# A gated block with sliding-window attention on one core: maxima and denominators go from SBUF to SBUF, and transfers that follow other engines are issued later

## The chip, the cores and the metric

The kernel runs on one core of a Trainium2 chip. The core has TensorE (matmuls, in the profile PE, its weight loads PEld), VectorE (DVE), ScalarE (ACT), GpSimd (POOL) and SyncE (SP), which issues nearly all transfers. [...] The metric is the device time of one execution in microseconds, the median of several runs.

## The reference

`x` is 2048 x 512. It is normalised by rows, and the result feeds two branches: causal attention over a window of 256 positions with 32 heads of 16, and a feed-forward network with a silu gate of width 1792. The output is the input plus attention times silu of the network's output.

```python
xn = _layernorm(x, axis=-1)
# s = _A_ref(xn, A_wqkv, A_wo)
scores = jnp.einsum("bhqd,bhkd->bhqk", q, k) * (Dh ** -0.5)
mask = (idx[:, None] - idx[None, :] >= 0) & (idx[:, None] - idx[None, :] < W)
scores = jnp.where(mask[None, None], scores, -1e9)
p = _softmax(scores, axis=-1)
o = jnp.einsum("bhqk,bhkd->bhqd", p, v)
return (lambda x, *d: x.transpose(*d))(o, 0, 2, 1, 3).reshape(B, S, D) @ wo
# g = _silu(_B_ref(xn, B_w1, B_w3, B_w2))
h = _silu(gate) * up
out = jnp.einsum("bsf,fd->bsd", h, w2)
# the output
return x + s * g
```

## The kernel before

**Tiles and units.** The 2048 positions are four blocks `t` of 512, the 32 heads four groups `g` of eight. A pair (t, g) is a *tile*; each tile has two *units* p of four heads, so there are 32 units, some 22 us each from the third on. Float32 accuracy is kept by splitting operands into two half-precision parts, hi and lo, and taking three products.

**Two passes a unit.** Pass 1 (L643) computes scores with queries on the partitions, adds the mask and takes the row maximum on VectorE (L675) into `M`. `negate` (L684) writes the negated maxima as two half-precision terms into `nm`. `finish` (L690) turns them on TensorE, VectorE copies them to `mt` (L700), and they become two more rows of the query tile `qa`, rows 64r+48 and 64r+49, so that the second score product subtracts the maximum by itself. `mt` is [32, 128], its rows in the order (term b, row half r, piece i). Pass 2 (L720) makes the scores again with the keys on the partitions (L741), masks them (L748), takes exp on ScalarE (L751), and multiplies with V, to which a column of ones is joined (L769): 16 rows of values and one of denominators for each head. `os` (L784, L785) collects these from PSUM, and its rows 16, 48, 80 and 112 are the denominators.

**From `os` to the attention output.** Four transfers (L791) gather the values of a unit into `on` [128, 512], head by head; one (L792) writes the denominators to a scratch tensor `dd` in HBM. When both units of a tile are done, `normalise` (L803) reads `dd` back as `dr` [128, 32] (L807), so that the reciprocal (L812, L813) runs over 128 partitions; the result goes to HBM as `de` (L815) and comes back eight times, broadcast to 16 partitions each, as `rb` (L819). GpSimd multiplies `on` by `rb` (L820, seen under the helper's line L339) and `cut` (L822) splits the product into the two parts that the output projection `total` (L1278, L1298) reads. `on`, `rb` and `os` have one buffer each, `qa` three.

**The feed-forward network** runs between the pieces of attention: `gate_up` (L1010, L1021), its products L1040 and L1045 on VectorE, the way down `down` (L1234, L1246) in blocks 0 and 1. In blocks 2 and 3 the way down is done with seven products in place of eight (`fold_first`, `fold_second`, `fold_down_piece`, L1164), on sums that GpSimd makes (L1079, L1102 to L1104); the folded weights are computed in block 1 by `fold_weights` (L960), written to `dFold` (L997) and read back by `load_fold` (L1141). Block 0 cuts each weight matrix into its parts and stores them in HBM, the later blocks load these (L849, L895, L628).

**What sets the order.** TensorE's instructions run in the order of the program text (`ORDERED`). For the other engines and for SyncE's queue, a scheduler picks the order when the program is built, by when it reckons that each instruction is ready and by priority; each engine then works strictly in that order, and waits at an instruction whose input has not come, with the rest of its queue behind it. `urgent()` (L138) raises the priority, `tc.issue_after` places an instruction behind a named one. The program text itself is a list of pieces of about six matmuls. `step()` (L148) counts them in `now`, and `later(n, f)` (L144) places the code of `f` n steps further on. A *slot* is a buffer of 2 KB a partition out of a pool of 55: `take` (L113) gives out the slot that was returned with the earliest time stamp, and `give(..., after=n)` (L120) stamps it n steps ahead, so that slots whose last reader is late are used again later. An instruction that writes a slot still waits for its last reader to be done.

The main loop (L1602) runs one unit after the other: pass 2 of unit n, with pass 1 of unit n + 2 and pieces of projections, values, output and network spread between. After each even unit, `fetch` (L630, L637, called at L1622) loads keys and queries of the tile whose pass 1 begins one unit later.

Of the kernel before, what the change touches and what calls it, by code (L numbers as in the profile page):

```python
# [51 lines left out]
VB = 10  # L52
SLOTS = 55
ORDERED = {ENGINE.PE}
# [29 lines left out]
def tile_block(ctx: ExitStack, tc: tile.TileContext, x, wqkv, wo, w1, w3, w2, out):  # L84
# [558 lines left out]
    def pass1(t, g, p):  # L643
# [40 lines left out]
        def negate():  # L684
            Mf = M.rearrange("p r a i -> p (r a i)")
            with tc.issue_after(lasts["emptied"].ins):
                nc.vector.tensor_scalar(nm[:, 0, :], Mf, -1.0 / ONE, None, op0=ALU.mult)
                nc.vector.scalar_tensor_tensor(nm[:, 1, :], Mf, -1.0 / ONE, nm[:, 0, :], op0=ALU.mult, op1=ALU.subtract)

        def finish(s):  # L690

            for h in range(2):
                rows = slice(64 * h, 64 * h + 64)
                nc.tensor.matmul(s[0:64, h, 448:512], whole[rows, 0:64], identh[rows, rows], start=True, stop=True)

            def rest():
                qa = QA[t, g]
                mt = small.tile([32, P], F16, name="mt")
                with urgent():
                    nc.vector.tensor_copy(mt.rearrange("p (h q) -> p h q", h=2), s[0:32, :, 448:512])  # L700
                dm = dpool.tile([32, P], F16, name="dm")
                nc.sync.dma_start(dm, mt)
                for r in range(2):
                    nc.sync.dma_start(qa[64 * r + KR:64 * r + KR + 2, 2 * p:2 * p + 2, :].rearrange("p a q -> p (a q)"),
                                      dm.rearrange("(b r i) q -> r b (i q)", b=2, r=2)[r])
            return rest
# [13 lines left out]
    def pass2(t, g, p):  # L720
# [54 lines left out]
        def finish():  # L775
# [3 lines left out]
            def rest():  # L779
# [6 lines left out]
                if p == 0:  # L786
                    ON[t, g] = (opool.tile([P, TW], F32, name="on", bufs=1), dpool.tile([8, TW], F32, name="dd"))
                on, dd = ON[t, g]
                for i in range(4):
                    h = (i // 2) * 4 + 2 * p + i % 2  # L790
                    nc.sync.dma_start(on[16 * h:16 * h + 16, :], os[32 * i:32 * i + 16, :])  # L791
                nc.sync.dma_start(dd[4 * p:4 * p + 4, :], os[DH::32, :])  # L792
                if p == 1:
# [9 lines left out]
    def normalise(t, g):  # L803
        on, dd = ON.pop((t, g))
        last = (t, g) == tiles[-1]
        dr = small.tile([P, 32], F32, name="dr")
        nc.sync.dma_start(dr, dd.rearrange("h (b c) -> (h b) c", c=32))  # L807
        rb = opool.tile([P, TW], F32, name="rb", bufs=1)

        def invert():  # L810
# [4 lines left out]
            nc.sync.dma_start(de.rearrange("h (b c) -> (h b) c", c=32), dr)  # L815
            for i in range(8):
                p, r, a = i // 4, i // 2 % 2, i % 2
                h = r * 4 + 2 * p + a
                nc.sync.dma_start(rb[16 * h:16 * h + 16, :], de[i:i + 1, :].to_broadcast([16, TW]))  # L819
            halves(nc.gpsimd.tensor_mul, on, on, rb)  # L820

# [138 lines left out]
    def fold_weights(j):  # L960
# [22 lines left out]
        def cut(raw, n, kind):  # L983
# [11 lines left out]
            def store():  # L995
                with behind_load():
                    nc.sync.dma_start(dFold[kind, :, j, 0:2 * n], a[:, 0:2 * n])  # L997
                give(a, after=30)
            later(8, store)

# [9 lines left out]
    def gate_up(t, f):  # L1010
        cell = {}

        def part(k, half):
# [28 lines left out]
            else:  # L1042
# [10 lines left out]
                def rest():  # L1053
                    nc.scalar.copy(hh[:, 0:TW], sg)  # L1054
                    halves(nc.gpsimd.tensor_sub, hh[:, TW:], sg, hh[:, 0:TW])
                    give(sg, after=8)
                later(1, rest)
# [220 lines left out]
    def total(t, b):  # L1278
# [4 lines left out]
        def part(half):  # L1283
# [16 lines left out]
            if half:  # L1300
# [4 lines left out]
                else:  # L1305
                    halves(nc.gpsimd.tensor_add, y, y, XR[t, b])
                nc.sync.dma_start(out[r, :], y)
                give(y, XR[t, b], after=6)
                if b == 3:
# [292 lines left out]
    for n, u in enumerate(units):  # L1602
# [18 lines left out]
        if n % 2 == 0 and k < len(tiles):  # L1621
            later(1, lambda k=k: fetch(*tiles[k]))  # L1622
    for b in (1, 3):
# [32 lines left out]
```

## Time and profile before

| | |
|---|---|
| Median of 3 runs | 815.16 us (814.53 to 816.15) |
| The profiled execution | 816.52 us, of which the span from first to last instruction is 814.7 us |
| Granted TensorE clock, mean | 0.999 |
| Moved by DMA | 134.71 MB, 165 GB/s over the span; the main queue took 55.6% of the 16 engines |
| Transfers issued by SyncE for maxima | 32 `dm<-mt` of 8 KB, 64 `qa<-dm` of 4 KB |
| for denominators | 32 `dd<-os` of 8 KB, 16 `dr<-dd` of 16 KB, 16 `de<-dr` of 16 KB |
| for values and factors | 128 `on<-os` and 128 `rb<-de`, 32 KB each |

How the rows of the profile are read: an engine's row names the line, what is written and read (`out<-in`), shapes and counts; "idle before" is the time in which that engine stood still ahead of the instruction, and the name behind the arrow is what ended it. SyncE computes nothing, so its rows are the issuing of transfers, and its waits are those of the whole queue. A matmul's busy time includes the part in which the next one already streams, so TensorE is marked busy a little longer than it is. Lines inside a helper stand for all its callers: L339 is every half-tile operation on GpSimd, and the tile names tell which.

### The profile page before, as it was taken

To read this page: it belongs to the slowest core of one execution; us is meant where nothing else is said; L and a number is where in the kernel's file an instruction comes from. 1 tells how busy PE (TensorE), PEld (TensorE's weight loads), DVE (VectorE), ACT (ScalarE), POOL (GpSimd) and SP (SyncE) were. 2 spreads that over 40 slices of the span, in tenths; PEclk is the share of its full clock that TensorE was granted. 3 is DMA by queue.
4 is the path that set the end of the run, shared out by engine and by line. 5 is a ranking of instruction groups with operands and counts; after the bars stand their busy time and mean duration, and the time that the engine had idled before them with its cause. 6 is when DMAs were issued, how large, how long until landed. Compare 5 with 4: busy or idle time off the path is not lost.

```text
span 814.7 us, 23924 instructions
## 1 busy us (share of the span) xinstructions
PE 794.2 (97%) x9176; PEld 404.0 (50%) x9176; DVE 636.6 (78%) x2037; ACT 392.5 (48%) x591; POOL 366.6 (45%) x648
## 2 busy tenths in 40 slices
PE   8999989999999999999999999999999999999997
PEld 4444444444444444444445444456544654466465
DVE  8788888888888768887988888586777887875537
ACT  6879596653546544345443443344344234344411
POOL 2234265333339447155253454530246276550671
PEclk9999999999999999999999999999999999999999
DMA  9979764666652576747556453755653653226511
GB/s 283 254 244 301 246 206 137 229 186 177 189 146 82 157 241 196 214 128 216 164 145 170 124 147 79 190 159 160 171 151 85 159 167 112 87 67 181 163 38 64
DMA packets 109923, 134.71 MB, mean 165 GB/s; under 512 B 18736, under 2 KB 64752, under 8 KB 109808
## 3 DMA queue, kind: packets, MB, share of 16 engines
q1 hardware_dynamic: 109520, 132.66, 55.6%
q8 instruction: 72, 1.18, 0.6%
q10 hardware_dynamic: 288, 0.52, 0.2%
q14 instruction: 43, 0.35, 0.1%
HBM read 91.75 MB, written 37.09 MB: 158 GB/s over the span
## 4 chain that ended last, share of the span: by engine, by line
PE 67%; DVE 12%; DMA 7%; ACT 6%; issue 3%; POOL 3%; SPq 1%; DVEq 0%; POOLq 0%; ACTq 0%
PE m L1021 25%; PE m L1164 8%; PE po L769 8%; PE m L1246 6%; PE m L593 6%; PE s L741 4%; DVE junk L675 3%; PE m L563 3%; PE m L1298 3%; PE s L661 2%; DVE s L748 2%; DMA slot<-dW 1%; PE po L661 1%; ACT pt L751 1%; DMA dm<-mt 1%
## 5 line engine op out<-in xcount | busy, mean ns | idle before, releaser
L1021 PE MATMUL m<-XH,slot 128*128 128x512 f16 x896 | 267.3, 380 | 1.9 <-DVE slot L614 1.2
L751 ACT ACTIVATE pt<-s,es 128x1024 f32<-128x1024 f32 x152 | 167.7, 1113 | 194.1 <-DVE s L748 182.6
L339 POOL TENSOR_TENSOR slot<-slot,slot 128x256 f16<-128x256 f32 (+1 forms) x170 | 113.3, 695 | 203.8 <-ACT slot L1054 75.6
L1021 PEld LDWEIGHTS <-slot 128*128 128x128 f16 x1344 | 124.9, 98 | 156.2 <-issue 12.6
L1021 PE MATMUL m<-XL,slot 128*128 128x512 f16 x448 | 169.8, 379 | 0.0
L748 DVE TENSOR_TENSOR s<-s,MK 128x256 f32<-128x256 f32 (+2 forms) x280 | 118.7, 434 | 50.9 <-PE s L741 45.7
L675 DVE CUSTOM_DVE_ANT_0 junk<-s,MW 128x320 bf16<-128x320 f32 x276 | 133.8, 485 | 17.6 <-PE s L661 10.2
L675 DVE CUSTOM_DVE_ANT_0 junk<-po,MW 128x320 bf16<-128x320 f32 x172 | 83.4, 485 | 4.2
L1246 PE MATMUL m<-slot,slot 128*128 128x512 f16 x336 | 78.7, 380 | 1.3 <-DVE slot L1040 0.9
L769 PE MATMUL po<-pt,V 64*32 64x320 f32 (+4 forms) x2880 | 77.2, 342 | 0.8 <-DVE pp L304 0.8
L593 PE MATMUL m<-XH,slot 128*128 128x512 f16 x240 | 70.9, 380 | 1.2 <-DVE slot L614 0.6
L1164 PE MATMUL m<-slot,slot 128*128 128x256 f16 x588 | 68.4, 273 | 0.0
L1079 POOL TENSOR_TENSOR slot<-slot,slot 128x256 f16<-128x256 f32 x98 | 64.7, 673 | 1.2
L1036 ACT ACTIVATE slot<-m,sgs 128x512 f32<-128x512 f32 x56 | 38.2, 683 | 54.8 <-PE m L1021 49.8
L1164 PEld LDWEIGHTS <-slot 128*128 128x128 f16 x588 | 56.2, 98 | 11.4 <-issue 2.8
L769 PEld LDWEIGHTS po<-pt,V 64*32 64x32 f32 x2880 | 50.4, 106 | 23.0 <-PE s L513 0.9
L1040 DVE SCALAR_TENSOR_TENSOR slot<-slot,m 128x512 f32<-128x512 f32 x56 | 38.3, 684 | 29.0 <-ACT slot L1036 28.9
L741 PE MATMUL s<-qa,KA 50*64 50x320 f16 (+3 forms) x1472 | 58.7, 259 | 1.8 <-DMA qa<-dm 1.7
L593 PEld LDWEIGHTS <-slot 128*128 128x128 f16 x384 | 35.7, 98 | 44.5 <-issue 3.2
L741 PEld LDWEIGHTS <-KA 50*64 50x64 f16 x1472 | 30.4, 105 | 53.8 <-issue 30.7
L339 POOL TENSOR_TENSOR on<-on,rb 128x256 f32<-128x256 f32 x32 | 24.4, 786 | 66.1 <-DMA rb<-de 58.1
L1246 PEld LDWEIGHTS <-slot 128*128 128x128 f16 x336 | 30.7, 98 | 39.7 <-issue 5.6
(188 smaller groups left out, 1121.9 us busy)
## 6 DMA issues: line engine op xcount, KB each, us to landing
slot<-dW SPq DMA_DIRECT2D x98, 256.0 KB
slot<-in_B_w_dram SPq DMA_DIRECT2D x56, 256.0 KB
slot<-dFold SPq DMA_DIRECT2D x48, 256.0 KB
dW<-slot SPq DMA_DIRECT2D x42, 256.0 KB
slot<-in_A_x_dram SPq DMA_DIRECT2D x30, 256.0 KB
KA<-dK SPq DMA_DIRECT2D x24, 288.0 KB
qa<-dQ SPq DMA_DIRECT2D x32, 192.0 KB
slot<-dWQ SPq DMA_DIRECT2D x24, 256.0 KB
```

Of the source, the lines that this page charges most:

```text
L339: op(out[:, c], a[:, c], b[:, c])
L593: nc.tensor.matmul(cell["pp"], w[:, (a * NC + c) * P:(a * NC + c + 1) * P], b[:, c, :], start=(c, i) == parts[0][0], stop=(c, i) == parts[ ...
L675: lasts["maximum"] = nc.vector.tensor_tensor_reduce(out=junk[:, :n], in0=s[:, r, :n], in1=mask, scale=1.0, scalar=NEG, op0=ALU.add, op1=AL ...
L741: nc.tensor.matmul(s[64 * h:64 * h + 64, r, o:o + 64 * n], ka[rows, 2 * p + a, 64 * (m + 4):64 * (m + 5)], qa[rows, 2 * p + a, 64 * (m + k ...
L748: nc.vector.tensor_add(v, v, MK[:, kind, of:of + n, :].unsqueeze(1).to_broadcast([P, 2 * len(which), n, 64]))
L751: lasts["exp"] = nc.scalar.activation(pt, s, AF.Exp, scale=es)
L769: nc.tensor.matmul(cell["po"][32 * i:32 * i + 32, h, 64 * (m + k):64 * (m + k + n)], V[64 * h:64 * h + 64, (4 * t + m // 2) % VB, hd * VW: ...
L1021: nc.tensor.matmul(cell[k], w[:, (a * NC + c) * P:(a * NC + c + 1) * P], b[:, c, :], start=c == 0 and i == 0, stop=c == NC - 1 and i == 2)
L1040: lasts["emptied"] = nc.vector.scalar_tensor_tensor(sg, sg, 1.0, cell[0], op0=ALU.add, op1=ALU.mult)
L1079: nc.gpsimd.tensor_sub(lo, view, hi)
L1164: nc.tensor.matmul(cell["ps"][:, c], made[:, f:f + P], wj[:, g:g + 256], start=j == j0 and c == 0 and n == 0, stop=j == j1 - 1 and n == 2, ...
L1246: nc.tensor.matmul(ps, hh[:, a * TW + b * P:a * TW + (b + 1) * P], w[:, c * D:(c + 1) * D], start=f == f0 and i == 0, stop=f == f1 - 1 and ...
```

## The change

Nothing is computed in another way; transfers and their places in the text change.

- *Maxima*: the scratch `dm` goes. Four transfers a unit, marked urgent, take eight rows of `mt` each and write one row of `qa`.
- *Denominators*: the scratch `dd` goes. `gather` copies the four rows of `os` straight into half of `dr` (64 partitions of 32 numbers) and then the values into `on`, two steps later than before except in the last tile.
- *Buffers*: `on` takes the pool's two buffers in place of one; the slots go from 55 to 54, which is as much memory.
- *Factors*: the loads of `rb` and the product come three steps after the reciprocal, except in the last tile.
- *Negations* are marked urgent.
- *Later*: stores of folded weights after 14 steps (8 before), output stores after four (at once before, and still so in the last block), `fetch` after three (one before). The gate's product gives its slot back 20 steps ahead in block 1 (8 before), output and residual 30 ahead (6 before).

```diff
-SLOTS = 55
+SLOTS = 54
...
         def negate():
             Mf = M.rearrange("p r a i -> p (r a i)")
-            with tc.issue_after(lasts["emptied"].ins):
+            with urgent(), tc.issue_after(lasts["emptied"].ins):
...
-                dm = dpool.tile([32, P], F16, name="dm")
-                nc.sync.dma_start(dm, mt)
-                for r in range(2):
-                    nc.sync.dma_start(qa[64 * r + KR:64 * r + KR + 2, 2 * p:2 * p + 2, :].rearrange("p a q -> p (a q)"),
-                                      dm.rearrange("(b r i) q -> r b (i q)", b=2, r=2)[r])
+                for b in range(2):
+                    for r in range(2):
+                        row = 64 * r + KR + b
+                        with urgent():
+                            nc.sync.dma_start(qa[row:row + 1, 2 * p:2 * p + 2, :].rearrange("p a q -> p (a q)"),
+                                              mt[16 * b + 8 * r:16 * b + 8 * r + 8, :])
...
                 if p == 0:
-                    ON[t, g] = (opool.tile([P, TW], F32, name="on", bufs=1), dpool.tile([8, TW], F32, name="dd"))
-                on, dd = ON[t, g]
-                for i in range(4):
-                    h = (i // 2) * 4 + 2 * p + i % 2
-                    nc.sync.dma_start(on[16 * h:16 * h + 16, :], os[32 * i:32 * i + 16, :])
-                nc.sync.dma_start(dd[4 * p:4 * p + 4, :], os[DH::32, :])
+                    ON[t, g] = opool.tile([P, TW], F32, name="on"), small.tile([P, 32], F32, name="dr")
+                on, dr = ON[t, g]
+
+                def gather():
+                    nc.sync.dma_start(dr[64 * p:64 * p + 64, :], os[DH::32, :])
+                    for i in range(4):
+                        h = (i // 2) * 4 + 2 * p + i % 2
+                        nc.sync.dma_start(on[16 * h:16 * h + 16, :], os[32 * i:32 * i + 16, :])
+                if (t, g) == tiles[-1]:
+                    gather()
+                else:
+                    later(2, gather)
...
     def normalise(t, g):
-        on, dd = ON.pop((t, g))
+        on, dr = ON.pop((t, g))
         last = (t, g) == tiles[-1]
-        dr = small.tile([P, 32], F32, name="dr")
-        nc.sync.dma_start(dr, dd.rearrange("h (b c) -> (h b) c", c=32))
...
-            for i in range(8):
-                p, r, a = i // 4, i // 2 % 2, i % 2
-                h = r * 4 + 2 * p + a
-                nc.sync.dma_start(rb[16 * h:16 * h + 16, :], de[i:i + 1, :].to_broadcast([16, TW]))
-            halves(nc.gpsimd.tensor_mul, on, on, rb)
+
+            def multiply():
+                for i in range(8):
+                    p, r, a = i // 4, i // 2 % 2, i % 2
+                    h = r * 4 + 2 * p + a
+                    nc.sync.dma_start(rb[16 * h:16 * h + 16, :], de[i:i + 1, :].to_broadcast([16, TW]))
+                halves(nc.gpsimd.tensor_mul, on, on, rb)
+            if last:
+                multiply()
+            else:
+                later(3, multiply)
...
-            later(8, store)
+            later(14, store)
...
-                    give(sg, after=8)
+                    give(sg, after=8 if t == 0 else 20)
...
-                nc.sync.dma_start(out[r, :], y)
-                give(y, XR[t, b], after=6)
+
+                def store():
+                    nc.sync.dma_start(out[r, :], y)
+                    give(y, XR[t, b], after=30)
+                if t == NT - 1:
+                    store()
+                else:
+                    later(4, store)
...
         if n % 2 == 0 and k < len(tiles):
-            later(1, lambda k=k: fetch(*tiles[k]))
+            later(3, lambda k=k: fetch(*tiles[k]))
```

## The prediction

> **What bounds the kernel now.** I read the engine totals first, then the same in stretches of 20 us, then the list of what TensorE waited for, then SyncE's queue and the chain of waits around the one place where a transfer holds TensorE.
>
> ```profile
> PE 794.2 (97%) x9176; PEld 404.0 (50%) x9176; DVE 636.6 (78%) x2037; ACT 392.5 (48%) x591; POOL 366.6 (45%) x648
> 100.00:120.00 20.00, 17.22 (x220) 8.50 (x219) 17.65 (x69) 17.13 (x33) 12.74 (x26) 1.00 0.65 204
> 500.00:520.00 20.00, 18.23 (x229) 8.50 (x228) 15.13 (x46) 7.87 (x10) 13.71 (x23) 1.00 0.46 123
> 520.00:540.00 20.00, 19.41 (x248) 9.85 (x246) 12.96 (x40) 7.81 (x11) 9.71 (x17) 1.00 0.64 179
> 800.00:815.00 15.00, 10.37 (x59) 5.32 (x57) 11.32 (x22) 2.73 (x5) 0.88 (x1) 0.94 0.20 72
> ```
>
> The stretches give span, then TensorE, its weight loads, VectorE, ScalarE and GpSimd, then clock, DMA share and GB/s. TensorE is busy for 794.2 of 814.7 us, its clock is full, and the number and order of its matmuls do not change here. So the change can win at most part of the 20.5 us in which TensorE is idle, and of these only what a transfer or a late VectorE step causes: some 2.8 us in 100 to 120, 1.8 in 500 to 520, 0.6 in 520 to 540, and the end.
>
> ```profile
> PE s L661 <- ACT pt L751: 2.1, 3, 1.0
> PE s L741 <- DMA qa<-dm: 1.7, 2, 1.5
> PE s L694 <- DVE NM L688: 1.2, 2, 1.1
> PE m L1298 <- DVE slot L827: 0.8, 1, 0.8
> PE s L661 <- DMA qa<-dQ: 0.4, 1, 0.4
> ```
>
> This view of waits (total us, times, longest) is the list of candidates. No weight load stands in it: TensorE never waits for a weight from HBM. The 1.7 us for the maxima is the one steady-state wait on a transfer, and it falls at 516 us:
>
> ```profile
> 499.82 0.27 DVE L700 CAST mt<-s 32x128 f16<-32x128 f32 x1
> 503.83 2.45 SPq L791 DMA_DIRECT2D on<-os  x4
> 509.19 0.36 SPq L1276 DMA_DIRECT2D slot<-in_A_x_dram  x1
> 510.70 0.38 SPq L702 DMA_DIRECT2D dm<-mt  x1
> ```
>
> The maxima are in SBUF at 500.1, and SyncE sends them at 510.7 only: its queue is in order, and `on<-os` ahead of them waits until 503.8 for GpSimd to be done with the one `on` buffer. The chain of waits carries on from there (start, us, what):
>
> ```profile
> 498.61 1.77 DMA rb<-de
> 510.70 2.97 DMA dm<-mt
> 513.99 2.85 DMA qa<-dm
> 523.88 3.14 DMA dd<-os
> 527.04 1.84 DMA dr<-dd
> ```
>
> Two hops in a row, 2.97 and 2.85, follow the late start and end at 516.84, under the scores of the next unit. The denominators then repeat it, 3.14 and 1.84. What SyncE itself waits for with its queue behind it:
>
> ```profile
> SPq L791 <- POOL slot L339: 34.1, 11, 5.4
> SPq L791 <- DVE os L785: 29.2, 6, 11.8
> SPq L704 <- DMA dm<-mt: 22.1, 16, 3.9
> SPq L819 <- DMA de<-dr: 19.9, 13, 3.8
> SPq L1141 <- POOL slot L1079: 15.1, 4, 10.8
> ```
>
> **The change part by part.** *Maxima.* The scratch `dm` goes; four transfers of one `qa` row each take the place of one write and two reads, marked urgent so that they go ahead in SyncE's order. That removes one hop (2.9 us) and the 22.1 us that SyncE spent waiting for `dm`.
>
> ```profile
> L704 SPq DMA_DIRECT2D qa<-dm x64: 228/251/336, 51.6 to 747.4; - x64
> L702 SPq DMA_DIRECT2D dm<-mt x32: 318/378/577, 49.0 to 745.2; - x32
> L791 SPq DMA_DIRECT2D on<-os x128: 507/581/1455, 86.4 to 783.9; - x128
> L792 SPq DMA_DIRECT2D dd<-os x32: 527/531/701, 89.7 to 784.5; - x32
> L819 SPq DMA_DIRECT2D rb<-de x128: 302/418/1680, 130.5 to 796.1; - x128
> ```
>
> Issuing was 32 x 0.378 + 64 x 0.251 = 28 us. A copy from 8 partitions into one row is not in the trace: between 0.251 (two rows) and 0.581 (16 rows from SBUF), so 128 of them cost 32 to 74 us. I take 0.53, the row from four partitions of SBUF, hence 68 us: 40 us more issuing against 22 us less waiting, spread over 32 units, about 0.6 us a unit on a queue that is not the bound. At 516 us it gives back the whole wait, 1.7 us: even if they were still held until 504, the rows would land at 504 + 4 x 0.53 + 3.0 = 509.1, while TensorE wants them 1.7 us before 516.84, at 515.1. Bounds: 0 (the urgent copies still stand behind another block until 510.7) to 1.7.
>
> [...] The row first: a hop here takes 1.77 to 3.14 us, whether it moves rows of 2 KB or of 128 bytes. [...]
>
> *Denominators.* `dd` goes; `dr` is filled straight from `os`, two copies a tile in place of three transfers: one issue less a tile, 16 x 0.38 = 6 us by the row of `dm<-mt`. Where a tile ends, one hop of 1.84 to 3.14 goes too, but the copies are put off by two steps (a step is some six matmuls, 6 x 0.22 = 1.3 us by the row of 25 below, so 2.6 us): even, except that SyncE no longer stands before an `os` that VectorE has not made (29.2 us above) and the reciprocal no longer stops VectorE:
>
> ```profile
> 528.90 0.35 DVE L812 RECIPROCAL dr<-dr 128x32 f32<-128x32 f32 x1 [3.33 <-DMA dr<-dd]
> ```
>
> Behind that reciprocal stand the masks, maxima and products of VectorE; TensorE pays for it near 533, in the 0.6 us of 520 to 540. I take 0.5 from 0 to 0.6.
>
> *Two `on` buffers, `rb` three steps later.* The 34.1 us of SyncE on the `on` buffer and the 19.9 us on `de` go. I cost both at nothing of their own: they are what makes the 1.7 us above safe. The eight `rb` loads and the product come some 4 us later; cover is the cut, due 14 steps (18 us) after the reciprocal, while three steps, eight issues and a landing take 3.9 + 8 x 0.42 + 1.77 = 9 us. Without cover TensorE would wait for the attention output up to the excess, at each of the three tiles that end a block.
>
> *The last tile.* Nothing is put off there, so the whole hop comes out:
>
> ```profile
> 782.07 2.42 SPq L791 DMA_DIRECT2D on<-os  x4
> 790.72 0.35 DVE L812 RECIPROCAL dr<-dr 128x32 f32<-128x32 f32 x1
> 798.00 2.88 POOL L339 TENSOR_TENSOR on<-on,rb 128x256 f32<-128x256 f32 x2 [4.80 <-DMA rb<-de]
> 799.47 2.72 PE L1298 MATMUL m<-slot,slot 128*128 128x512 f16 x11
> 802.21 0.68 DVE L827 TENSOR_TENSOR slot<-on,slot 128x512 f16<-128x512 f32 x1
> 802.95 5.57 PE L1298 MATMUL m<-slot,slot 128*128 128x512 f16 x25 [0.75 <-DVE slot L827]
> ```
>
> The denominators leave first, at 782.1, and land by 785.3 at the latest (3.14) instead of under a reciprocal at 790.7: five us earlier, or some two if VectorE takes the reciprocal later in its order. The product then starts at 793 to 796, not 798. TensorE's interval is (5.57 - 0.38)/24 = 0.216, its twelfth matmul would start at 799.47 + 11 x 0.216 = 801.85 and did at 802.95: 1.1 us, of which I take 1.0 (0 if the product stays behind GpSimd's other work).
>
> *Negations.* They are made urgent:
>
> ```profile
> 112.22 0.97 DVE L475 TENSOR_SCALAR slot<-slot,mv,rs 128x512 f32<-128x512 f32 x1
> 113.11 0.64 DVE L688 SCALAR_TENSOR_TENSOR NM<-M,NM 128x16 f16<-128x16 f32 x1
> ```
>
> The second negation stood behind a 0.97 us centring, and TensorE waited 1.1 us for it. VectorE is busy for 17.65 us of that stretch, so what it does first delays the rest, and L751 waits follow: I take 0.6 of the 1.2, from minus 0.3 to 1.2.
>
> *Stores, loads and releases later.* Output stores wait four steps, folded weights 14 instead of 8, `fetch` three instead of one, and slots rest longer, with one slot less. Cover for `fetch` is the whole unit between it and the first use (TensorE's only wait for `qa<-dQ` is 0.4 us, once); without it 2.6 us for each of 14 tiles. Slots are the risk, since loads that take a young slot wait for its last reader; I put 0.5 us on them and on the new order of VectorE, from minus 1 to plus 8 (the slot rival).
>
> **Sum**: minus 1.7, 0.5, 1.0 and 0.6, about 0.1 for smaller reciprocal stalls, plus 0.5: minus 3.4 us. The profiled execution took 816.52 with a span of 814.7 and 1.8 around it, so it would become 813.1; it stands 1.36 above the median of 815.16, which becomes 811.8.
>
> **Rivals.** *The next wait takes over.* The early stretch shows how: behind the wait for the negation stands the one for L751, 2.1 us in all. Only the end and a third of the rest would be kept: 1.0 + 0.9 - 0.5 = 1.4 less, 813.8, within what a measurement can tell from no change, which is 0.2%, 1.6 us. For it: VectorE and ScalarE are over 17 of 20 us busy at 100. Against: at 500 to 540 they are at 13 to 15 and 8.
>
> *Slots become too young (slower).* The place is the loads of folded weights before L1164:
>
> ```profile
> 717.81 0.34 SPq L1141 DMA_DIRECT2D slot<-dFold  x1
> 721.77 1.45 PE m L1164 x12
> ```
>
> SyncE stood 10.8 us before this load for a GpSimd cut (L1079); it lands at 717.81 + 2.97 = 720.8, one us before the stage it serves begins. With 54 slots and releases up to 24 steps later, such a load gets a slot whose reader ends later. If the 10.8 grows by half, TensorE loses 5.4 - 1.0 = 4.4 us; two of the four fold stages give 8.8, and 811.8 - 0.5 + 8.8 is about 820. It decides from 1 us of extra lateness, and makes the kernel slower than before when the losses pass 3.9. For it: the 15.1 us of such waits. Against: the added rests fall on slots that GpSimd reads late, and steer loads away from these.
>
> *The whole early part gains as well.* If SyncE's freedom also feeds ScalarE and VectorE in the first 200 us, half of the 2.8 us at 100 to 120 and the same again elsewhere go: 3 us more, 808.8.
>
> *The copies do not come first.* If the urgent mark does not move them, the wait at 516 stays at its lower bound: 813.5; it counts with the first rival.
>
> **How the numbers follow.** Forecast 0.51, next wait (with the last) 0.21, slots 0.18, early part 0.10. Faster than 813.5 holds in nearly all of the forecast and the early part and in a little of the second: 0.61. The same: most of the second, 0.18. Slower than 816.8: the slots and the rest, 0.21. The range takes 808.8 below and reaches above to 817.5, into the smaller half of the slot case; the forecast's own, by the bounds of its terms, is 809.5 to 814.
>
> **What would show it.** Right: no wait of TensorE on `qa` at 500 to 520, no idle VectorE before L812, no row of SyncE waiting for L339 at the gather, and the product `on<-on,rb` of the last tile before 797. Wrong: TensorE waiting for slots in L1164 or L1021, `qa<-mt` landing over 5 us after its first issue, or an idle sum in 100 to 200 that grows by what the end gives.

## The result and the profile after

The changed kernel takes 818.0 us (median of 20 runs, 816.36 to 819.84), the kernel before 814.88 us beside it (20 runs, 813.24 to 819.63): a ratio of 1.0037, interval 1.0027 to 1.0047. It is 3.1 us slower, where 3.4 us less were predicted, and outside the predicted range. The profiled execution took 817.82 us with a span of 816.0. Executions of one kernel differ here: of the twenty of the changed kernel, three with a mean clock of 1.000 took 816.36 to 816.39 us and seventeen with 0.996 or 0.998 took 817.49 to 819.84, so each ratio below is against runs of the kernel before on the same chip, whose medians go from 813.98 to 817.77.

The engine totals of the changed kernel, and the same stretches as before (span, TensorE, its weight loads, VectorE, ScalarE, GpSimd, clock, DMA share, GB/s), with 180 to 200 beside them:

```profile
PE 795.2 (97%) x9176; PEld 404.2 (50%) x9176; DVE 633.9 (78%) x2037; ACT 392.4 (48%) x591; POOL 364.0 (45%) x648
```

and the stretches:

```profile
100.00:120.00 20.00, 16.39 (x178) 7.69 (x178) 17.67 (x69) 15.72 (x30) 12.07 (x26) 1.00 0.62 198
180.00:200.00 20.00, 16.80 (x135) 7.13 (x129) 12.35 (x46) 4.51 (x5) 5.30 (x16) 0.91 0.50 151
500.00:520.00 20.00, 19.93 (x253) 9.44 (x251) 15.51 (x52) 8.43 (x12) 13.39 (x23) 1.00 0.35 105
520.00:540.00 20.00, 20.00 (x190) 9.65 (x186) 14.33 (x44) 9.44 (x13) 8.72 (x15) 1.00 0.73 202
```

500 to 540 has become as full as predicted. 100 to 120 lost another 0.8 us. The new hole is at 180 to 200, where the kernel before had TensorE busy for 19.61 us, and there the clock is no longer full. The same two places head the list of what TensorE waited for (total, times, longest):

```profile
PE m L1257 <- DVE slot L614: 3.2, 1, 3.2
PE s L661 <- ACT pt L752: 2.9, 3, 1.6
```

The first wait is a single one. GpSimd around it, in the kernel before:

```profile
183.94 0.20 POOL L466 TENSOR_TENSOR sq<-sq,u 128x4 f32<-128x4 f32 x1
184.23 0.22 POOL L467 TENSOR_SCALAR sq<-sq 128x4 f32<-128x4 f32 x1
...
185.65 0.20 POOL L472 TENSOR_TENSOR rs<-sq,r 128x4 f32<-128x4 f32 x1
185.98 1.59 POOL L339 TENSOR_TENSOR on<-on,rb 128x256 f32<-128x256 f32 x2
```

and in the changed one (timelines: start, duration, what, and in brackets the idle time before and what ended it):

```profile
185.47 0.20 POOL L466 TENSOR_TENSOR sq<-sq,u 128x4 f32<-128x4 f32 x1
185.80 1.42 POOL L339 TENSOR_TENSOR on<-on,rb 128x256 f32<-128x256 f32 x2
187.30 0.22 POOL L467 TENSOR_SCALAR sq<-sq 128x4 f32<-128x4 f32 x1
187.58 0.40 POOL L841 CAST slot<-on 128x256 f16<-128x256 f32 x1
...
189.37 0.67 POOL L339 TENSOR_TENSOR slot<-on,slot 128x256 f16<-128x256 f32 x1
190.12 0.19 POOL L471 TENSOR_SCALAR sq<-sq 128x4 f32<-128x4 f32 x1
190.40 0.20 POOL L472 TENSOR_TENSOR rs<-sq,r 128x4 f32<-128x4 f32 x1
```

VectorE there:

```profile
190.63 0.55 DVE L475 TENSOR_SCALAR slot<-slot,mv,rs 128x512 f32<-128x512 f32 x1 [3.40 <-POOL rs L472]
191.09 0.68 DVE L614 SCALAR_TENSOR_TENSOR slot<-m,slot 128x512 f16<-128x512 f32 x1
```

TensorE there:

```profile
191.83 2.72 PE L1257 MATMUL m<-slot,slot 128*128 128x512 f16 x6 [3.20 <-DVE slot L614]
```

The same matmuls in the kernel before (L1246 there):

```profile
187.64 1.46 PE L1246 MATMUL m<-slot,slot 128*128 128x512 f16 x6 [0.39 <-DVE slot L614]
```

In the changed kernel the next stretch, by engine, has a clock of 0.50 (third from the end):

```profile
191.56:194.98 3.42, 3.15 (x20) 1.13 (x23) 0.87 (x2) 0.00 (x0) 0.00 (x0) 0.50 0.66 207
```

L463 to L472 are ten small steps on 128 x 4 numbers, which refine the inverse deviations `rs` of block 2. Before, they ran in one go and the product `on<-on,rb` of a tile came behind. Now the product and the cut stand between them, and `rs` comes 4.9 us after L466 instead of 1.7. VectorE's centring (L475) waits for it 3.40 us, behind it the step (L614) that empties a bank of PSUM, the memory into which the matmuls write, and TensorE 3.20 us for the bank. Then comes a stretch of 3.42 us at half clock: six matmuls take 2.72 us, where they took 1.46 before.

The end went as predicted. GpSimd starts the last product at 795.23, not 798.00, and TensorE's wait inside L1309 (L1298 before) is 0.21 us:

```profile
795.23 1.41 POOL L339 TENSOR_TENSOR on<-on,rb 128x256 f32<-128x256 f32 x2
807.07 2.75 PE L1309 MATMUL m<-slot,slot 128*128 128x512 f16 x12 [0.21 <-DVE slot L1313]
```

### The profile page after: what moved, and what is told of

Same layout as the page of the kernel before. It is cut to its first block, busy times and chain, and to the rows that moved or that the text cites. A ratio compares the mean times of both kernels' runs of the same rounds, so it can differ in the third digit from the quotient of the medians.

```text
span 816.0 us, 23868 instructions
## 1 busy us (share of the span) xinstructions
PE 795.2 (97%) x9176; PEld 404.2 (50%) x9176; DVE 633.9 (78%) x2037; ACT 392.4 (48%) x591; POOL 364.0 (45%) x648
## 3 DMA queue, kind: packets, MB, share of 16 engines
q8 instruction: 72, 1.18, 0.6%
## 4 chain that ended last, share of the span: by engine, by line
PE 78%; DVE 10%; ACT 5%; DMA 3%; issue 3%; SPq 1%; POOL 1%; DVEq 0%; POOLq 0%; ACTq 0%
PE m L1032 29%; PE po L770 8%; PE m L1257 8%; PE m L1175 8%; PE m L593 7%; PE s L742 5%; PE m L1309 4%; PE m L563 4%; PE s L661 3%; DVE junk L675 2%; PE po L661 2%; DMA slot<-in_A_x_dram 1%; DMA dW<-slot 1%; DVE s L749 1%; ACT slot L342 1%
## 5 line engine op out<-in xcount | busy, mean ns | idle before, releaser
L1032 PE MATMUL m<-XH,slot 128*128 128x512 f16 x896 | 267.5, 380 | 1.8 <-DVE slot L614 1.2
L1032 PEld LDWEIGHTS <-slot 128*128 128x128 f16 x1344 | 124.8, 98 | 156.2 <-issue 12.7
L1032 PE MATMUL m<-XL,slot 128*128 128x512 f16 x448 | 169.9, 379 | 0.0
L675 DVE CUSTOM_DVE_ANT_0 junk<-s,MW 128x320 bf16<-128x320 f32 x276 | 133.9, 485 | 18.0 <-PE s L661 10.3
L675 DVE CUSTOM_DVE_ANT_0 junk<-po,MW 128x320 bf16<-128x320 f32 x172 | 83.4, 485 | 4.3
L1175 PE MATMUL m<-slot,slot 128*128 128x256 f16 x588 | 68.4, 273 | 0.0
L1175 PEld LDWEIGHTS <-slot 128*128 128x128 f16 x588 | 56.1, 98 | 11.5 <-issue 2.8
L661 PE MATMUL s<-KA,qa 48*64 48x320 f16 (+3 forms) x824 | 45.1, 295 | 3.7 <-ACT pt L752 2.9
```

Of the source, the lines that this page charges most:

```text
L661: nc.tensor.matmul(s[c:c + w, r, :n], qa[rows, 2 * p + a, ii * P + c:ii * P + c + w], ka[rows, 2 * p + a, e - n:e], start=True, stop=True)
L675: lasts["maximum"] = nc.vector.tensor_tensor_reduce(out=junk[:, :n], in0=s[:, r, :n], in1=mask, scale=1.0, scalar=NEG, op0=ALU.add, op1=AL ...
L1032: nc.tensor.matmul(cell[k], w[:, (a * NC + c) * P:(a * NC + c + 1) * P], b[:, c, :], start=c == 0 and i == 0, stop=c == NC - 1 and i == 2)
L1175: nc.tensor.matmul(cell["ps"][:, c], made[:, f:f + P], wj[:, g:g + 256], start=j == j0 and c == 0 and n == 0, stop=j == j1 - 1 and n == 2, ...
```

## The experiments

**Order or late product? (one step count).** Two theories at first: the order of GpSimd's queue makes the loss (order theory), or SyncE's longer issuing and the slots do. In e1 the loads of `rb` and the product come after eight steps, which makes the scheduler keep the ten small steps together. e2 leaves the transfers of before alone and only delays `rs`, by two operations that nobody reads; the product of a tile then falls between the later small steps too.

```diff
 e1 (on the change)
-                later(3, multiply)
+                later(8, multiply)
 e2 (on before): two GpSimd operations on 128 x 256 between L466 and L467, block 2 only
```

> The changed kernel with one number altered: the product of a tile comes eight steps after the reciprocal, not three. Theory (GpSimd's queue): at 185 us the changed kernel has the product and the cut of a tile between the small steps L467 to L472 of block 2's normalisation, so the centring L475 stops VectorE, L614 behind it is late, and TensorE stands for 3.2 us and then runs 3.4 us at half clock; with eight steps the small steps come first, so about 4.7 us go: 818.0 becomes 813 to 814, ratio to before 0.998 to 0.999. Rival (late releases and stores, slots): the stall is one of many and another takes its place: 817 to 818, ratio 1.003 to 1.004.

> The kernel before, with two extra GpSimd operations of 128x256 between the small steps of block 2's normalisation, whose results nobody reads; in the order that this gives, the product of a tile falls between the later small steps too. Nothing else of the change is in it. Theory (GpSimd's queue): the last small step is late by some 3.4 us, TensorE stands for 2 to 3 us at 190 us and loses clock: 817 to 819.5, ratio 1.003 to 1.006. Rival (slots): a late GpSimd there is hidden; within 1 us of before, ratio 0.999 to 1.001.

e1: 813.36 us (12 runs, 812.94 to 813.89), ratio 0.9947 (0.9926 to 0.9968) against 817.77 of the kernel before on that chip; in its profile no stall at 190, clock 1.00, span 812.1. e2: 821.86, more than the 817 to 819.5 expected, with its ratio of 1.0053 (1.0022 to 1.0084) inside what was expected, and the changed kernel's hole in the kernel before:

```profile
PE m L1252 <- DVE slot L620: 3.4, 1, 3.4
```

L620 is L614 there. A late `rs` is enough for the stall of 3.4 us and for the loss of clock (0.91 in 180 to 200, as in the change); a product that stays behind it takes both away.

**Which part brings the order.** e3 holds the new transfers of maxima and denominators (issued where they were) and the urgent negations; e4 all the rest with the scratch tensors kept, and `dr<-dd` three steps later, which is an edit of its own; e7 the maxima alone, e8 maxima and denominators.

> The kernel before with three of the edits: maxima from SBUF to SBUF, denominators from SBUF to SBUF (issued where they were), negations urgent; one buffer for the product, 55 slots, every store and release where it was. Theory (GpSimd's queue): the scheduler reckons with fewer hops, so it puts the product between the small steps here too: TensorE waits some 3 us for L614 at 190 us, and the time is 816.5 to 818.5, ratio 1.002 to 1.0045. Rival (slots, late stores): none of that is in it, so only the gains are: 811.5 to 814, ratio 0.996 to 0.999.

> The complement: the kernel before with two buffers for the product, 54 slots, the gather two steps later, the product three steps later, stores, fetch and releases later; maxima and denominators still through HBM, negations as before. Theory (GpSimd's queue): the small steps stay together, no stall at 190 us, 813.5 to 815.5, ratio 0.998 to 1.001. Rival (slots, late stores): the loss is here, 817 to 819, ratio 1.003 to 1.005.

> The kernel before with the maxima alone from SBUF to SBUF and urgent. Both theories say that GpSimd's small steps stay together here. If the prediction's term for the maxima holds, the wait of TensorE for the maxima at 516 us (1.7 us) is gone and the time is 1 to 2.5 us under the kernel before on the same chip, with less scatter, since its slow executions would be those in which SyncE's queue is late. If SyncE's other blocks still hold the urgent copies, it is within 0.7 us of it.

> The kernel before with maxima and denominators from SBUF to SBUF, negations as before. In this order the product falls between the small steps too, but later among them (two steps and the cut's copies ahead of L472). Theory (GpSimd's queue): L472 is late by about 2.5 to 3 us, TensorE stands for 2 to 2.8 us near 190 us; 1 to 3 us slower than the kernel with the maxima alone. Rival (the loss comes from the negations): no stall there, as fast as the maxima alone or faster by the end's 1 us.

| | us | ratio (interval) | TensorE's largest new wait |
|---|---|---|---|
| e3 | 818.95 | 1.0018 (0.9997 to 1.004) | 3.2 for L614 at 188 to 192 |
| e4 | 819.75 | 1.0023 (0.9997 to 1.005) | 2.7 for the gate's product (L1055) at 755 |
| e7 | 831.79 | 1.0211 (1.0191 to 1.0231) | 9.7 for a projection weight at 396 |
| e8 | 817.2 | 1.0029 (1.0011 to 1.0048) | 2.8 for L614 at 190 |

The times of e3 and e4 are not clear of the kernel before on that chip; what tells them apart is the order on GpSimd. In e3 and e8 the product stands between the small steps, in e4 and e7 behind them. So the shorter way for the denominators together with that for the maxima brings the order, with the product's code where it was (e3, e8) as well as three steps later (the change); neither of them brings it alone (e7, and e10 below), nor do the buffers, the slots and the three steps (e4). e4 missed the 813.5 to 815.5 expected of it, by a stall of its own: VectorE stands 4.71 us before a reciprocal that waits for `dr<-dd`.

e7 fits no theory of then. TensorE's timeline in it, then SyncE's:

```profile
396.00 1.04 PE L593 MATMUL m<-XH,slot 128*128 128x512 f16 x2 [9.73 <-DMA slot<-dWQ]
```

```profile
379.57 0.39 SPq L850 DMA_DIRECT2D slot<-dW  x1
389.00 0.34 SPq L1308 DMA_DIRECT2D out_dram<-slot  x1
...
393.56 0.38 SPq L628 DMA_DIRECT2D slot<-dWQ  x1
```

What SyncE waited for there (total, times, longest), and GpSimd's row:

```profile
SPq L1308 <- POOL slot L339: 8.2, 1, 8.2
```

```profile
387.57 2.66 POOL L339 TENSOR_TENSOR slot<-slot,slot 128x256 f32<-128x256 f32 x4
```

An output store stands 8.2 us at the head of SyncE's queue, for a residual sum of GpSimd that runs at 387.57; the weight behind it arrives late. In the kernel before that sum runs ahead of ten operations on folded weights (L979 to L992), in e7 behind them:

```profile
380.40 1.41 POOL L339 TENSOR_TENSOR slot<-slot,slot 128x256 f32<-128x256 f32 x2
381.76 0.73 POOL L979 TENSOR_TENSOR slot<-slot,slot 128x256 f32<-128x256 f32 x1
```

By these rows it is again the order on GpSimd, at another place.

e11 puts the output stores ten steps later in e7's kernel, so that the store follows the weight.

> The kernel with the maxima alone, and in it the output stores of the first three blocks ten steps later (and y given back 30 ahead). The maxima alone took 831.8 us, with TensorE waiting 9.7 us at 386 to 396 for a projection weight that stands behind an output store in SyncE's queue; the store waits for a sum of GpSimd. Here that store comes behind the weight. Theory of the queue: both waits for dWQ (9.7 and 1.3 us) are gone, no half clock at 388, and the time is 813 to 816, about what the kernel before needs, less up to 1.7 for the wait at 516 if it is gone too. Rival, contention (the new copies of 256 bytes slow the weight's landing): the wait stays at 5 us or more and the time over 824.

Measured: 817.13 us (12 runs, 815.37 to 825.6), ratio 1.0047 (1.0023 to 1.0071), some 14 us below e7 on another chip. The wait is 2.7 us in its profile, so the queue was most of it and not all: the time is above the 813 to 816 expected.

**The change again, and its order alone.** e6 leaves the transfers, buffers, slots, negations and loads of `rb` as the change has them, and puts only the product later: five steps further on in all tiles but the last, and behind L472.

```diff
-            pool.tensor_mul(rs[:, b0:b1], sq, r0)
+            lasts["rs"] = pool.tensor_mul(rs[:, b0:b1], sq, r0)
...
-                halves(nc.gpsimd.tensor_mul, on, on, rb)
+                later(0 if last else 5, product)
+
+            def product():
+                with nullcontext() if last else tc.issue_after(lasts["rs"].ins):
+                    halves(nc.gpsimd.tensor_mul, on, on, rb)
```

> The changed kernel as it is, so that it and the next three stand on one chip beside the kernel before. Theory (GpSimd's queue): TensorE waits 3 us for L614 near 190 us, 3.4 us at half clock follow, 817 to 819. Rival (slots, late stores): the same time, but with waits spread over 400 to 700 us.

> The changed kernel with GpSimd's order put right and nothing else meant to move: the loads of the factors stay three steps after the reciprocal, only the two half-tile products come five steps further on and behind the last small step (L472) of the normalisation that was traced last. Theory (GpSimd's queue): the wait for L614 at 190 us and the half clock go, 812.5 to 814.5, some 4.5 us under the changed kernel on this chip. Rival (the factor loads on SyncE, which the first experiment moved as well, made the difference): no better than the changed kernel, 817 to 819.

On one chip: before 814.22, the change 817.05 (ratio 1.0037, 1.0022 to 1.0052), with the order mended 813.82 (ratio 0.9993, 0.9981 to 1.0005), its span 812.1 against 816.6. GpSimd in e6:

```profile
187.34 0.20 POOL L472 TENSOR_TENSOR rs<-sq,r 128x4 f32<-128x4 f32 x1
187.66 1.59 POOL L339 TENSOR_TENSOR on<-on,rb 128x256 f32<-128x256 f32 x2
```

By the medians the order costs 3.2 us, all of the slowdown (some 4.5 was expected). The change's median stands between two groups there: three executions of 816.28 to 816.46 us with a mean clock of 1.000, three of 817.64 to 818.47 with 0.998. So the order costs some 2.6 us without the half clock and some 4.3 with it. But the mended kernel is level with before, not 3.4 us below it, and the rest of the study is about that.

**Single parts on one chip.** e9 is the kernel before with urgent negations, e10 with the denominators from SBUF to SBUF, e12 is e1's kernel again.

> The kernel before with the negations urgent and nothing else. The prediction put 0.6 us on them (minus 0.3 to 1.2). If that holds: TensorE's wait for NM is 1.2 us shorter in all, the span is 0.3 to 0.9 below that of the kernel before, and the time 0.2 to 0.8 us below it, with no stall of over 2 us anywhere. If urgent work on VectorE only moves a delay, the NM wait is gone and other waits of TensorE between 100 and 140 us grow by the same 1 us: the time is that of the kernel before within 0.3 us.

> The kernel before with the denominators copied from os into dr, issued where they were before, and nothing else. The prediction put 0.5 us on the reciprocal's stalls and 1.0 on the last tile. If both hold by themselves: no idle VectorE of over 1 us before the reciprocal L811 or so, the wait in 800 to 810 under 0.3 us, time 1.0 to 1.8 below before. The small steps of block 2's inverse deviations keep together on GpSimd here, so the order theory expects no stall at 190 us. If instead SyncE's queue turns out to be what counts, a new wait of TensorE for a load of over 1 us appears and the gain is not seen.

> The change with the product eight steps behind the reciprocal, once more, on another chip if there is one. It took 813.4 where the kernel before took 817.8, which is more than that kernel takes elsewhere (814 to 815). Order theory: 812.9 to 813.9 again, with no wait of TensorE over 1.7 us and the clock at 1.00, and below the kernel before by 0.7 to 1.8 us where that takes 814 to 815.

Before took 813.98. e9: 816.7, ratio 1.0034 (1.0013 to 1.0054), a loss where both theories had none. e10: 813.07, ratio 0.9985 (0.9972 to 0.9997), 0.9 us less where 1.0 to 1.8 were expected. e12: 813.27, ratio 0.9989 (0.9975 to 1.0004), as expected. The new waits of e9:

```profile
PE s L661 <- ACT pt L751: 3.0, 3, 1.6
PE po L661 <- DVE M L675: 0.9, 1, 0.9
```

The wait for `NM` is gone, and two others have grown. At 77 us VectorE takes a row maximum (L675) later than before, and TensorE waits 0.90 us for it. At 120 us the exp of L751 is later, for the order of ScalarE's queue moved too: a sum of squares (L249), which in the kernel before starts four us ahead of that exp, now stands right ahead of it. ScalarE in e14 (the kernel before, see below), then in e9:

```profile
112.68 0.63 ACT L249 ACTIVATE sqa<-slot 128x512 bf16<-128x512 f32 x1
...
116.92 1.10 ACT L751 ACTIVATE pt<-s,es 128x1024 f32<-128x1024 f32 x1
```
```profile
118.55 0.62 ACT L249 ACTIVATE sqa<-slot 128x512 bf16<-128x512 f32 x1
119.08 0.19 ACT L249 ACTIVATION_READ_ACCUMULATOR sqa<-slot 128x1 f32 x1
119.17 1.09 ACT L751 ACTIVATE pt<-s,es 128x1024 f32<-128x1024 f32 x1
```

**Is the profile of before typical?** e13 and e14 are the kernel before, unchanged, profiled twice more; e15 is e12 with the negations as before.

```diff
 e15 (on the change)
-            with urgent(), tc.issue_after(lasts["emptied"].ins):
+            with tc.issue_after(lasts["emptied"].ins):
...
-                later(3, multiply)
+                later(8, multiply)
```

> The kernel before, unchanged, for a second profile of it. In e9 the transfers are those of before and in the same order from 450 us on, yet TensorE's matmuls there gain 2.0 us between 480 and 520 and 0.6 by 535 on the first profile of before, as they do in every other kernel. If the wait of 1.7 us for qa at 516 and the late reciprocal near 533 were chance of that one execution (its hop de<-dr at 489 took 4.86 us): this profile shows neither, a span of 812 to 813, and the wait list without qa<-dm over 0.7 us. If they are a regular part of before: TensorE waits 1 us or more for qa<-dm at 510 to 520 again and the span is 814 to 815.

> The kernel before once more, a third profile: as e13. Chance would show in the waits for qa<-dm and in the hops de<-dr differing between the three profiles; a regular wait would be in all three at the same place.

> The change with the product eight steps behind the reciprocal and the negations not urgent. The step stretch 60 to 120 us, in which the urgent negations cost TensorE 1.4 to 1.6 us (against the 0.6 us gain that the prediction put on them), should run as in before. Theory: 811.7 to 812.7, about 1 us below e12 and 1.3 to 2.2 below before, with the wait for NM of 1.2 us there again. Rival, that the negations cost nothing in this company: 813.0 to 813.5, as e12.

e13 took 816.4 us (10 runs; ratio 1.0012, 0.9991 to 1.0033), with a profiled span of 814.2, above the 812 to 813 that chance alone was expected to leave; e14, one execution, 814.15 with a span of 812.4. e15 took **811.74 us** (12 runs, 811.40 to 812.17; before 815.16 on that chip), ratio 0.9941 (0.9917 to 0.9964): it beats the kernel before, and by its ratio the change. The stretch 500 to 520 of e13 and e14, and 520 to 540 of each:

```profile
500.00:520.00 20.00, 19.93 (x251) 9.31 (x249) 15.76 (x47) 8.37 (x12) 12.89 (x23) 1.00 0.39 110
520.00:540.00 20.00, 18.82 (x236) 10.01 (x233) 13.01 (x43) 7.09 (x9) 10.15 (x18) 1.00 0.70 190
```
```profile
500.00:520.00 20.00, 19.93 (x253) 9.35 (x252) 15.78 (x48) 8.55 (x12) 12.21 (x22) 1.00 0.53 136
520.00:540.00 20.00, 19.72 (x250) 10.44 (x250) 14.23 (x47) 7.79 (x10) 11.62 (x21) 1.00 0.63 169
```

The hole of 500 to 520 that the first profile showed (18.23) is in neither. Most of it was made by one hop: `de<-dr` took 4.86 us there (from 489.01), while in e14 the loads of `rb` follow its issue by 492.04 - 488.61 = 3.4 us; issuing these eight loads then took 5.14 us against 4.57. But e14 waits for the maxima at another place, 424.6 us, and e13 nowhere:

```profile
PE s L741 <- DMA qa<-dm: 0.6, 1, 0.6
```

Since TensorE runs the same 9176 matmuls in the same order in all these kernels, the start of the same matmul can be subtracted. The table gives each profile minus e14, in us, at the matmul that e14 starts at the given time:

```
at               60    140    195    480    540    790    end
before, first +0.37  +0.63  +0.63  +0.02  +2.37  +2.37  +2.37
e13           +0.26  +0.27  +0.27  -0.19  +1.37  +1.85  +1.85
the change    +0.28  +1.94  +6.30  +4.91  +4.58  +4.43  +3.68
e6            +0.41  +2.09  +2.31  +0.93  +0.60  +0.45  -0.29
e9            +0.59  +2.24  +2.40  +1.08  +0.83  +0.83  +0.84
e10           +0.38  +0.64  +0.62  -0.08  -0.42  -0.42  -1.16
e12           +0.40  +2.05  +1.70  +0.33  +0.00  -0.14  -0.88
e15           +0.27  +0.26  -0.22  -1.55  -1.89  -2.04  -2.79
```

Read by columns: from 60 to 140 the kernels with urgent negations lose 1.6 to 1.7 us, those without lose 0.3 or nothing. From 140 to 195 only the change loses much, 4.36 (e6 0.22, e9 0.16). From 195 to 480 all others gain on e14, those with the transfers of before too (first profile 0.61, e9 1.32). e14 has three waits there: 0.30 us at 238, 0.21 at 318 and the 0.59 at 425 for the maxima. So much of this part belongs to e14's execution, and the table can't say what of it is due to an edit. From 790 to the end every kernel with the new denominators gains 0.75.

## Why the prediction was wrong

**The step that failed** is the price of the new order. The prediction costs the product's new place "at nothing of their own" and allows 0.5 us for slots, stores and "the new order of VectorE"; GpSimd's order has no term. It followed the data and asked whether the product comes too late. It did not ask what becomes of the queue in which the product stands if its data are expected earlier, which is what the parts on maxima and denominators bring by taking out a hop each. With these hops gone the scheduler gave the product an earlier place, between the steps of `rs`, in an engine that is 45% busy. The passage with "nothing of their own" is on two buffers and three steps, and these are not the cause: e3 and e8 have the stall without them, e4 has them without it. The missing term measured 4.36 us from 140 to 195: 2.80 of added waiting (3.20 where e14 waits 0.40), 1.48 in the stretch at half clock and 0.08 ahead of both. e6 shows it by the order alone: 0.22 us there.

**Negations** had the wrong sign: plus 1.66 us (60 to 140) where minus 0.6, at worst plus 0.3, was written. The rival *the next wait takes over* named L751 as the next wait, and it did grow, from 1.0 to 1.6 us at 120. But that rival only took the gain away. It had no term for a loss by the new orders of VectorE and ScalarE: in e9 another 0.57 us go between 60 and 85, with the wait of 0.90 for L675. The gain was overrated as well. Of the 1.1 us for `NM` in the first profile, e14 has 0.46: the step L298 ahead of it took 0.70 us in the one and 0.16 in the other.

**Maxima, 1.7 us at 516.** The wait is gone from the changed kernel, so the mechanism was right, but the wait is not steady: the three profiles of before have 1.7 us at 516, 0.6 at 425 and none, so there was less to give, 0.8 us on the mean of the three. What held the transfer last was not the `on` buffer either: a load of folded weights (L1141), which had waited for GpSimd's L1079, was issued right ahead of it.

```profile
510.29 0.33 SPq L1141 DMA_DIRECT2D slot<-dFold  x1
```

The prediction set its sum against the profiled execution, which stood 1.36 us above the median, and then took the whole sum off the median. The issue cost was outside its bounds too, without harm: 128 x 0.644 = 82 us against 32 to 74.

```profile
L705 SPq DMA_DIRECT2D qa<-mt x128: 634/644/1341, 48.9 to 746.8; - x128
```

**Denominators.** TensorE's loss near 533 goes in the change (20.00 at 520 to 540), and it is 0.59, 1.18 and 0.28 us in the three profiles of before. But e9, with the old denominators, is at 19.97 there and e1, with the new ones, at 19.69, so it is not shown that this gain is the edit's. "No idle VectorE before L812" did not come true: the reciprocal (L817 now) still ends a gap, though TensorE does not stand for it.

```profile
531.02 0.35 DVE L817 RECIPROCAL dr<-dr 128x32 f32<-128x32 f32 x1 [2.67 <-DMA dr<-os]
```

The hop that was taken out won no time at this place. In seven traces with the new denominators this reciprocal waits for its copy, and it starts 5.8 to 7.8 us after the copy was issued (7.2 in the change, from 523.86). With the two hops of before it is 5.0 to 5.3 us in the three profiles. Near 745 it is the other way: 2.0 to 2.4 us with the one hop, 4.8 to 5.2 with the two. What makes the one hop long near 525 is not shown.

**Small pieces** did not make the hop of the maxima long: in e7 one that writes 256-byte pieces (a row of `mt`) took 1.72 us, where the two hops of before took 2.97 and 2.85. With pieces of 128 bytes (a row of `dr`) e1 has a hop of 5.95 us near 525; but in the change the reciprocal near 745 starts 2.28 us after a copy in the same pieces, so their size alone does not make the long hop. The rows of the chains of waits, e7 and then e1:

```profile
70.44 1.72 DMA qa<-mt
```

```profile
521.21 5.95 DMA dr<-os
```

**The last tile** was right: the product started at 795.23 (793 to 796 was written), although all of the changed kernel ran some 2 us later by then, and the end gives 0.75 us where 1.0 was taken.

**The rivals.** *Slots too young* did not happen: TensorE waits for no load at L1175 or L1032, and e4, which has the new slots and releases, has none either. *The whole early part gains* was the reverse of what happened. The slower case was given 0.21, for a mechanism that was not the one at work.

**One sum** of the prediction does not come out. By the bounds of its own terms the forecast reaches to 0.3 - 0.1 + 0.5 = 0.7 us above the median, 815.9, and not only to 814.

**Luck.** e15 takes 3.4 us less than the kernel before, the very time that was forecast for the change. That does not bear out the sum: e15 has no urgent negations, and by the table it is 0.26 us behind e14 at 140 and then gains 0.48 up to 195, 1.33 up to 480, 0.34 and 0.15 up to 790, and 0.75 at the end.

**What stays open**: which edits give the gains between 195 and 480; why one hop of the denominators takes so long near 525; what causes e11's remaining 2.7 us; and why the kernel before and the negations alone scatter more from run to run than e1, e6, e12 and e15 do (on one chip 812.69 to 819.3 us for the kernel before, 814.43 to 821.93 for e9, 813.11 to 813.94 for e12).

## What to carry to other kernels

Where a scheduler orders the queues, an edit that lets a result come earlier can also move the work that uses it, and an engine that is half idle can then hold a short chain on which the critical engine depends (here GpSimd, 45% busy, made `rs` 4.9 us after L466 instead of 1.7, and TensorE waited 3.20 us): look in each queue for the chains that must not be split, and hold them together. A gain that is read from a single wait in a single profile should be sought in a second profile first; if the profiled execution is above the median, some of its waits may be chance (the 1.7 us for the maxima were 0.6 and none in the two other profiles of before). Making one thing urgent on a full engine can take the time from others, and can move the orders of other queues with it (in e9 the wait for L751 at 120 us went from 1.0 to 1.6 us).

## What the hardware showed

The clock fell to half after idle times of TensorE of 3.20 us (the change) and 2.66 us (e4, below), for 3.42 and 3.41 us. It did not fall after 1.6 us (e9, 1.00 from 119 to 127) and 2.28 us (e7, where the six matmuls behind the wait took 1.46 us). After 4.1 us (e11, below) the mean of 250 to 262 was 0.74, by which some 6.2 us of these 12 were at half, an estimate. The fall does not come each time: six of 26 executions of the change have a mean clock of 1.000 and took 816.3 to 816.5 us; none of these was traced. TensorE's row in e4 and the stretch behind it:

```profile
755.21 0.59 PE L1036 MATMUL m<-XH,slot 128*128 128x512 f16 x2 [2.66 <-DVE slot L1055]
```

```profile
755.74:759.15 3.41, 3.41 (x37) 1.20 (x42) 0.76 (x2) 0.00 (x0) 2.45 (x4) 0.50 0.17 36
```

One small instruction took some twenty times its median duration. In the profile of e11, an execution of 825.6 us, a negation of 128 x 16 numbers took 6.13 us (median 0.304), TensorE waited 4.1 us behind it, and the mean clock of 250 to 262 was 0.74. GpSimd ran ten operations on 128 x 256 without a gap from 248.12 to 254.42; the negation ended at 254.45. The 17 traces hold 544 of these negations. The 202 that ran while GpSimd stood still took 0.16 to 0.18 us, and each of the 290 that took over 0.2 us ended 0.03 to 0.04 us after a GpSimd operation did. All but this one ended after the first or the second operation; why this one passed ten is not shown. The line's shortest, median and longest time in ns, the negation and the last eight operations of GpSimd, and that stretch:

```profile
L687 DVE TENSOR_SCALAR NM<-M x32: 165/304/6135, 45.4 to 748.1; 128x16 f16<-128x16 f32 x32
```

```profile
248.32 6.13 DVE L687 TENSOR_SCALAR NM<-M 128x16 f16<-128x16 f32 x1
249.38 5.04 POOL L339 TENSOR_TENSOR slot<-slot,slot 128x256 f16<-128x256 f32 x8
```

```profile
250.00:262.00 12.00, 7.88 (x39) 2.89 (x37) 9.97 (x21) 3.64 (x5) 6.59 (x12) 0.74 0.36 115
```
